# A two-phase attention and feed-forward kernel: one weight reload issued later and from another queue, denser weight conversion between the phases, and another order of the last products

## The chip, the cores and the metric

The kernel runs on one core of one Trainium2 chip. The metric is the device time of one execution, in microseconds (us), as a median of several runs. The core has a matrix engine (PE, with its weight loads shown apart as PEld), VectorE (DVE), ScalarE (ACT), GpSimd (POOL) and SyncE (SP, which here only issues DMA transfers). Each engine works through its own instructions in their order and waits for the others by semaphores.

## The reference

Sliding-window attention with a few sink columns, then a feed-forward layer over all 3072 tokens:

```python
scores = scale * np.matmul(q, k.transpose(0, 1, 3, 2))      # 4 x 8 heads, 768 x 768, head size 64
scores = np.where(is_sink | in_window, scores, -1e9)
a = softmax(scores)
x = np.matmul(a, v)            # -> 3072 tokens x 512
h = x @ w_in                   # 512 -> 2048
r = np.maximum(h, 0.0)
g = s * (r * r) + b
out = g @ w_out                # 2048 -> 512
```

The weights arrive as 8-byte floats, which the kernel turns into float32 itself, and every float32 number is split into a high and a low part for the matrix engine.

## The kernel before

**Two phases.** In the first, the tokens go through in 8 chunks of 384: attention and the first layer together. For each chunk, 16 column blocks of `h` (f = 0 to 15) are made from 12 matmuls each (L692), ACT takes each block through Relu into a tile `g` (L698), and each pair of blocks is stored to DRAM (L700, from SP). `g` has three buffers, so the ACT instruction of a pair waits until the store of the pair three before it has landed. In the second phase the 3072 tokens go through in 6 blocks (`blk`) of 512, and each block in 8 steps (`q`), together 48 units `n`. A unit loads a pair of `h` blocks back (`load`, L778, from SP), squares and combines it on ACT and DVE into the operands `gA` and `gH` (`prep`, L780 to L799), and PE multiplies them with seven combinations of the second layer's weights into seven accumulators `Q[j]` (`products`, L817): 42 matmuls, in the order j = 0, 1, 5, 6, 4, 2, 3. j = 0, 1 and 3 take `gA`, the other four `gH`. `prep(n+1)` is written ahead of `products(n)`.

**The weights of the second layer.** Step q needs a tile `v{q}` of converted weights. Six of the eight pairs are converted early, among the attention chunks. Three of them stay in SBUF; the other three (q = 3, 4, 5) are stored to DRAM (`spilled`) and fetched back when the attention's buffers are free: `reload(q)`, L763, 1792 KB each, called here reload 3, 4 and 5. The last two raw weight words (q = 6 and 7, 1024 KB each, called raw 6 and raw 7) are loaded (L709, SP) at that moment into the tiles that reloads 4 and 5 will later fill, and converted while PE works on the last chunk's `h`. The conversion of one (`w2_steps`) is two ACT instructions on the raw words (L235, L236), three DVE instructions (L237, L239, L241), DVE differences (L718) and casts on ACT (L721, L734). It is written in four pieces, one behind each `h` block from the third on (`late_w2`, in the loop over the last chunk), and reload 4 or 5 stands behind each conversion.

**What sets the order.** A scheduler sets the order of instructions on each engine from the order in which they are written and from its own estimates, so pieces that are written later may still stand between others. SP's transfers start in SP's order.

**The end.** In the last step of a block, `drain` adds the accumulators up: `u1` is a copy of `Q[0]` (ACT, L834), `o1`'s left half is `Q[1] + u1`, `u1 += Q[5]`, `u3 = Q[6] + u1`, `u1 += Q[4]`, `o2`'s right half is `Q[4] + u3`, `o1`'s right half is `Q[2] + u1` (DVE, all by the helper at L830), and `o2`'s left half is `u3 - Q[3]`, in the last block in two parts with a bank each (L822). In the last block each part is sent off by `put` (L862, SP) as soon as it is written.

Of the kernel before, what the change touches and what calls it, by code (L numbers as in the profile page):

```python
# [8 lines left out]
F32 = mybir.dt.float32  # L9
F32R = mybir.dt.float32r  # L10
I32 = mybir.dt.int32
U32 = mybir.dt.uint32
U8 = mybir.dt.uint8
AF = mybir.ActivationFunctionType
ALU = mybir.AluOpType
AX = mybir.AxisListType

P = 128
B, H, S, D = 4, 8, 768, 64
# [15 lines left out]
EARLY, SPILL = 3, 3  # L35
HD = DM // 2
NP = NF // 2
TB = 4 * P
NT = B * S // TB
# [6 lines left out]
def tile_kernel(ctx, tc, qT, kT, k0, v, vsk, n_sink, window, w1, w2, s, b, out):  # L46
    nc = tc.nc
# [6 lines left out]
    def ps(name):  # L54
        return pools[0].tile([P, 512], F32, tag="a", name=name)
# [3 lines left out]
    kept = kept_cm.__enter__()  # L59
# [54 lines left out]
    rel, rel1, low, upp, kix, snk, tmp, tm2 = (sc0[:, j, :] for j in range(8))  # L114
# [97 lines left out]
    weight, raws, last = {}, {}, {}  # L212
# [12 lines left out]
    def scratch(name, dt=F32):  # L225
        return kept.tile([P, 2, DM], dt, tag="cs", name=name, bufs=2)

    def float_steps(raw, scratch, pin=lambda x: x, up=2.0 ** -111):


        lo, hi = raw[..., 0], raw[..., 1]
        t = []
        sc, ve = nc.scalar, nc.vector
        return [
            lambda: pin(sc.activation(lo, lo.bitcast(U32), AF.Copy, scale=2.0 ** -29)),  # L235
            lambda: pin(sc.mul(hi.bitcast(F32), hi.bitcast(F32), up)),  # L236
            lambda: pin(ve.tensor_scalar(out=t.append(scratch()) or t[0], in0=hi, scalar1=3, scalar2=None,  # L237
                                         op0=ALU.logical_shift_left)),
            lambda: pin(ve.scalar_tensor_tensor(out=t[0], in0=hi, scalar=-0x80000000, in1=t[0],  # L239
                                                op0=ALU.bitwise_and, op1=ALU.bitwise_or)),  # L240
            lambda: pin(ve.tensor_tensor(out=hi, in0=t[0], in1=lo, op=ALU.add))]  # L241
# [463 lines left out]
    spilled = {q: dram.tile([P, 7, 2, HD], F32R, tag=f"wd{q}", name=f"wd{q}") for q in range(EARLY, EARLY + SPILL)}  # L705
# [31 lines left out]
    def halves_of(t):  # L737
        return t[:, :3], t[:, 3:]
# [15 lines left out]
    def second_layer(p2):  # L754


        def late_v(q, shape=(P, 7, 2, HD), dt=F32R):
            return p2.tile(list(shape), dt, tag=f"v{q}", name=f"v{q}")

        def reload(q):  # L760
            t = late_v(q)
            wc[q] = halves_of(t)
            nc.gpsimd.dma_start(t, spilled[q])  # L763

        for q in range(2):
            load_w2(NP - 2 + q, late_v(EARLY + 1 + q, [P, 2, 2 * DM], I32))
        reload(EARLY)
        wc[NP - 2] = halves_of(late_v(NP - 2))
        wc[NP - 1] = (p2.tile([P, 3, 2, HD], F32R, tag="vb", name="vb"), kept_w(0, "vt", [P, 4, 2, HD], F32R))

# [30 lines left out]
        Q = {}  # L801

        def products(n):
            blk, q = units[n]
            left = ready.pop(n)
            right = [wc[q][0][:, j] for j in range(3)] + [wc[q][1][:, j] for j in range(4)]
            last, end = q == NP - 1, blk == NT - 1
            for j in (0, 1, 5, 6, 4, 2, 3):
                if q == 0:
                    Q[j] = ps("Q").rearrange("p (r f) -> p r f", r=2)  # L810
                    if end and j == 3:
                        Q[3, 1] = ps("Q").rearrange("p (r f) -> p r f", r=2)
                for rb in range(2):
                    parted = end and j == 3
                    bank = Q[3, 1] if parted and rb else Q[j]
                    for i, (gi, wi) in enumerate(((0, 0), (0, 1), (1, 0))):
                        nc.tensor.matmul(bank[:, rb], left[j][:, gi, rb * P:(rb + 1) * P], right[j][:, wi],  # L817
                                         start=(q == 0 and (rb == 0 or parted) and i == 0),
                                         stop=(last and (rb == 1 or parted) and i == 2))
                    if last and parted:  # L820
                        o = D["o"][1]
                        nc.vector.tensor_tensor(out=o[:, rb, :HD], in0=D["u3"][:, rb], in1=bank[:, rb], op=ALU.subtract)  # L822
                        put(blk, 1, o, slice(rb, rb + 1), slice(0, HD))
                if last and not parted:
                    drain(blk, j)

        D = {}

        def drain(blk, j):
            add = lambda o, x, y, op=ALU.add: nc.vector.tensor_tensor(out=o, in0=x, in1=y, op=op)  # L830
            u = lambda name: kept.tile([P, 2, HD], F32, tag="x0", name=name, bufs=2)
            if j == 0:
                D["u1"] = u("u1")
                nc.scalar.copy(D["u1"], Q[0])  # L834
                D["o"] = [kept.tile([P, 2, DM], F32, tag="x1", name="ot", bufs=2) for _ in range(2)]
            o1, o2 = D["o"]
            end = blk == NT - 1
            lo, hi, both = slice(0, HD), slice(HD, DM), slice(0, 2)
            if j == 1:
                add(o1[:, :, lo], Q[1], D["u1"])  # L840
                if end:
                    put(blk, 0, o1, both, lo)
            if j == 5:
                add(D["u1"], Q[5], D["u1"])
            if j == 6:
                D["u3"] = u("u3")
                add(D["u3"], Q[6], D["u1"])
            if j == 4:
                add(D["u1"], Q[4], D["u1"])
                add(o2[:, :, hi], Q[4], D["u3"])  # L850
                if end:
                    put(blk, 1, o2, both, hi)
            if j == 2:
                add(o1[:, :, hi], Q[2], D["u1"])
                put(blk, 0, o1, both, hi if end else slice(0, DM))
            if j == 3:
                nc.vector.tensor_tensor(out=o2[:, :, lo], in0=D["u3"], in1=Q[3], op=ALU.subtract)
                put(blk, 1, o2, both, slice(0, DM))

        def put(blk, half, o, rb, cols):  # L860
            rows = out[blk * TB + half * HT:blk * TB + (half + 1) * HT, cols].rearrange("(r p) e -> p r e", p=P)
            nc.sync.dma_start(rows[:, rb], o[:, rb, cols])  # L862
# [193 lines left out]
    todo = [(max(t * t1 - LEAD, 0.3), f) for t, f in enumerate(plain)] + [(t2 - 2, constants3), (t2, scalars)]  # L1056
# [17 lines left out]
    reload, load, prep, products, n_units = second_layer(p2)  # L1074
    late = {}

    def late_w2(q, a, z):
        if a == 0:
            late[q] = w2_steps(q)
        for f in late[q][a:z]:  # L1080
            f()

    todo = []
    for j in range(2):
# [2 lines left out]
    for m in range(n, len(steps)):  # L1087
        steps[m]()
        if m % PIECES < PIECES - 1:
            continue  # L1090
        m = m // PIECES - n_last
        if m == NF // 2:
            go = out_of_range()
        if m >= 2 and todo:
            todo.pop(0)()
        if m >= NF - 3:
            load(m - (NF - 3))
    prep(0)
# [57 lines left out]
```

## Time and profile before

| what | us |
|---|---|
| median of 3 runs | 726.9 (726.4 to 727.88) |
| the profiled execution | 726.22 |
| its span, first to last instruction | 724.5 |
| PE busy | 696.1 (96%) |
| PE weight loads busy | 659.1 (91%) |
| DVE busy | 575.6 (79%) |
| ACT busy | 531.7 (73%) |
| POOL busy | 130.5 (18%) |

The profiled execution is 1.7 us longer than its span and 0.7 us under the median of the runs. PE is busy nine tenths of nearly every slice of the span; the shares of the others say little about a single stage. The change touches two stages: the turn from phase 1 to phase 2, about 436 to 487 us from the span's start, and the last 12 us. For these the views to read are who waited for whom on PE, the chain of work that ended last, the instructions in order of time, and the transfers with their time to landing.

### The profile page before, as it was taken

How to read it: one execution, taken by the hardware profiler on the slowest of the kernel's cores; microseconds unless marked ns; L12 is line 12 of the kernel's file. 1: busy time of each engine (PE TensorE's matmuls, PEld its weight loads, DVE VectorE, ACT ScalarE, POOL GpSimd, SP SyncE). 2: the span in 40 equal slices, each digit the busy share in tenths (PEclk: the TensorE clock that was granted, in tenths of full speed). 3: DMA queues.
4: the chain of work that ended last, by engine and by line, in shares of the span. 5: the costliest groups of instructions: out<-in, count | busy, mean ns of one | idle time of the engine just before them, and what ended most of it. 6: DMA issues, size and time to landing. Idle time of an engine off the chain costs nothing.

```text
span 724.5 us, 14198 instructions
## 1 busy us (share of the span) xinstructions
PE 696.1 (96%) x4858; PEld 659.1 (91%) x4858; DVE 575.6 (79%) x1458; ACT 531.7 (73%) x1229; POOL 130.5 (18%) x295
## 2 busy tenths in 40 slices
PE   9889999999999999999999999999999999999995
PEld 5667789999999998898899999999999999999995
DVE  7798976977887887877977862858888888888883
ACT  5898788789789789888888853846566665756561
POOL 4000122424424424424324310000000000000000
PEclk9999999999999999999999999999999999999998
DMA  8942254366456456453454318863534444443521
GB/s 206 410 148 84 67 180 149 107 209 219 133 178 222 141 169 244 126 175 112 136 185 131 108 67 327 267 221 117 154 109 124 138 118 146 117 146 117 151 84 62
DMA packets 61185, 114.13 MB, mean 158 GB/s; under 512 B 8368, under 2 KB 37168, under 8 KB 58288
## 3 DMA queue, kind: packets, MB, share of 16 engines
q1 hardware_dynamic: 59584, 107.43, 46.1%
q0 software_dynamic: 432, 5.51, 2.2%
q8 instruction: 40, 0.66, 0.4%
q14 instruction: 41, 0.34, 0.1%
q10 hardware_dynamic: 1088, 0.20, 0.1%
HBM read 76.16 MB, written 36.96 MB: 156 GB/s over the span
## 4 chain that ended last, share of the span: by engine, by line
PE 40%; DVE 14%; ACT 7%; DMA 7%; issue 4%; POOL 0%; ACTq 0%; DVEq 0%; POOLq 0%; SPq 0%
PE Q L817 21%; PE h L692 14%; DMA gs<-gs 5%; PE o L405 2%; DVE gA L796 2%; DVE sm L344 1%; DMA kraw<-in_kT 1%; ACT sm L350 1%; DVE hl L369 1%; ACT gs L785 1%; DVE gH L798 1%; DVE kl L321 1%; DVE u L830 1%; DVE qs L320 1%; ACT g L698 1%
## 5 line engine op out<-in xcount | busy, mean ns | idle before, releaser
L692 PE MATMUL h<-x,w 128*128 128x384 f32 x1536 | 306.4, 343 | 4.4 <-DVE negm L344 2.9
L692 PEld LDWEIGHTS h<-x,w 128*128 128x128 f32 x1536 | 261.9, 188 | 11.6 <-DVE negm L344 4.6
L817 PE MATMUL Q<-v,gH 128*128 128x256 f32 x1008 | 128.5, 283 | 0.3 <-DVE ot L830 0.2
L817 PEld LDWEIGHTS Q<-v,gH 128*128 128x128 f32 x1008 | 124.2, 192 | 0.7 <-issue 0.6
L785 ACT ACTIVATE gs<-gs,sbu 128x1024 f32<-128x1024 f32 x48 | 55.3, 1151 | 70.1 <-DMA gs<-gs 63.2
L817 PE MATMUL Q<-v,gA 128*128 128x256 f32 x756 | 99.0, 283 | 1.1 <-DVE gA L796 1.1
L350 ACT ACTIVATE sm<-sm,negm 128x264 f32<-128x264 f32 (+1 forms) x144 | 72.8, 506 | 32.3 <-DVE negm L344 28.8
L817 PEld LDWEIGHTS Q<-v,gA 128*128 128x128 f32 x756 | 94.4, 192 | 1.4 <-DVE gA L796 1.3
L698 ACT ACTIVATE g<-h 128x384 f32<-128x384 f32 x128 | 62.2, 490 | 18.6 <-PE h L692 13.3
L352 POOL COPY psk<-sm 128x24 f32<-128x24 f32 x144 | 37.0, 259 | 177.8 <-ACT sm L350 176.0
L369 DVE TENSOR_TENSOR hl<-tp,hl 128x256 fp32r<-128x256 f32 (+1 forms) x144 | 57.9, 403 | 9.7 <-ACT hl L368 8.7
L344 DVE CUSTOM_DVE_ANT_0 sm<-sc,msk 128x264 f32<-128x264 f32 (+1 forms) x144 | 59.0, 410 | 3.7 <-PE sc L340 1.2
L798 DVE TENSOR_TENSOR gH<-gs,gH 128x1024 fp32r<-128x1024 f32 x48 | 58.4, 1217 | 2.8 <-ACT gH L797 2.8
L795 ACT ACTIVATE gA<-gs,sbu 128x512 fp32r<-128x512 f32 x96 | 53.7, 607 | 8.3 <-PE Q L817 8.3
L405 PE MATMUL o<-hl,vv 128*128 128x128 f32 (+2 forms) x352 | 56.5, 278 | 3.4 <-DVE hl L369 1.7
L797 ACT CAST gH<-gs 128x1024 fp32r<-128x1024 f32 x48 | 50.0, 1041 | 12.1 <-DVE gs L790 7.0
L796 DVE SCALAR_TENSOR_TENSOR gA<-gs,sbu,gA 128x512 fp32r<-128x512 f32 x96 | 54.8, 611 | 0.0
L414 DVE TENSOR_TENSOR xm<-o,y 64x384 f32<-64x384 f32 x48 | 26.6, 555 | 34.3 <-ACT y L413 31.0
L787 DVE SCALAR_TENSOR_TENSOR gs<-gs,sbu 128x256 f32<-128x256 f32 x48 | 23.1, 482 | 37.9 <-ACT gs L785 37.7
L368 ACT CAST hl<-tp 128x256 fp32r<-128x256 f32 (+1 forms) x144 | 50.7, 353 | 1.7 <-PE tp L364 1.0
L405 PEld LDWEIGHTS o<-hl,vv 128*128 128x128 f32 (+1 forms) x352 | 40.3, 164 | 6.1 <-DVE hl L369 2.7
L339 PE MATMUL sc<-kh,qs 128*128 128x264 f32 (+1 forms) x144 | 40.2, 279 | 0.8 <-ACT g L698 0.6
(180 smaller groups left out, 1154.5 us busy)
## 6 DMA issues: line engine op xcount, KB each, us to landing
gs<-g SPq DMA_DIRECT2D x64, 384.0 KB, 3.1
gs<-gs SPq DMA_DIRECT2D x48, 512.0 KB, 4.2
kraw<-in_kT SPq DMA_DIRECT2D x32, 264.0 KB, 2.8
wraw<-in_w SPq DMA_DIRECT2D x8, 1024.0 KB, 11.4
vraw<-in_w SPq DMA_DIRECT2D x6, 1024.0 KB, 5.4
wd<-v SPq DMA_DIRECT2D x3, 1792.0 KB, 6.4
v<-wd POOLq DMA_DIRECT2D x3, 1792.0 KB, 9.5
out<-ot SPq DMA_DIRECT2D x10, 512.0 KB, 3.2
```

The source lines that it names most:

```text
L344: nc.vector.tensor_tensor_reduce(out=sm[:, :n], in0=sc[:, :n], in1=m, scale=-0.125, scalar=BIG, op0=ALU.add, op1=ALU.min, accum_out=negm[: ...
L350: nc.scalar.activation(sm[:, :n], sm[:, :n], AF.Exp, bias=negm[:, uu], scale=-1.0, accum_out=pp.zz[:, i, hh:hh + 1])
L368: nc.scalar.copy(hi, tp[:, a:z])
L369: nc.vector.tensor_tensor(out=lo, in0=tp[:, a:z], in1=hi.bitcast(F32), op=ALU.subtract)
L405: nc.tensor.matmul(hd.o[:m, q0:q0 + n * P], hd.vv[:, kb, :m], hd.hl[:, t, c0 * P:(c0 + n) * P], start=(hd.n == 0), stop=(end and t == 0))
L692: nc.tensor.matmul(h[:, :CH], w_in(f, wi)[:, cc * P:(cc + 1) * P], k.x[xi][:, cc, :], start=(i == 0), stop=(i == len(order) - 1))
L698: nc.scalar.activation(g["r"][:, f % 2], h[:, :CH], AF.Relu, scale=1.0 / WUP)
L785: nc.scalar.activation(g[:, 0], g[:, 0], AF.Square, scale=root_ap)
L795: nc.scalar.activation(o[:, :, 0], x, AF.Identity, bias=b1_ap, scale=1.0)
L796: stt(out=o[:, :, 1], in0=x, scalar=b1_ap, in1=o[:, :, 0].bitcast(F32), op0=ALU.add, op1=ALU.subtract)
L798: nc.vector.tensor_tensor(out=H[:, :, 1], in0=S, in1=H[:, :, 0].bitcast(F32), op=ALU.subtract)
L817: nc.tensor.matmul(bank[:, rb], left[j][:, gi, rb * P:(rb + 1) * P], right[j][:, wi], start=(q == 0 and (rb == 0 or parted) and i == 0), s ...
```

## The change

Four things. The reload of q = 3 is no longer issued by POOL before the last chunk; it is issued from ACT's queue, behind the first ACT instruction on raw 7 (and as plain float32, on both sides). The pieces of the last two conversions are called denser: one behind the third `h` block, then two behind each of the next three. In the last block the products go in the order j = 0, 5, 6, 4, 1, 2, 3. And there `Q[1]` is copied by ACT and added by POOL, from a tile with three parts, instead of by DVE.

```diff
-            lambda: pin(sc.activation(lo, lo.bitcast(U32), AF.Copy, scale=2.0 ** -29)),
+            lambda: last.update(low=pin(sc.activation(lo, lo.bitcast(U32), AF.Copy, scale=2.0 ** -29))),
...
-        def reload(q):
+        def reload(q, queue=nc.gpsimd):
             t = late_v(q)
             wc[q] = halves_of(t)
-            nc.gpsimd.dma_start(t, spilled[q])
+            queue.dma_start(t.bitcast(F32), spilled[q].bitcast(F32))
...
-        reload(EARLY)
...
-            for j in (0, 1, 5, 6, 4, 2, 3):
+            for j in (0, 5, 6, 4, 1, 2, 3) if end else (0, 1, 5, 6, 4, 2, 3):
...
             if j == 0:
-                D["u1"] = u("u1")
+                if blk == NT - 1:
+                    us = kept.tile([P, 3, 2, HD], F32, tag="x0", name="us", bufs=2)
+                    D["u1"], D["sum"], D["q1"] = (us[:, i] for i in range(3))
+                else:
+                    D["u1"] = D["sum"] = u("u1")
...
             if j == 1:
-                add(o1[:, :, lo], Q[1], D["u1"])
                 if end:
+                    nc.scalar.copy(D["q1"], Q[1])
+                    nc.gpsimd.tensor_tensor(out=o1[:, :, lo], in0=D["q1"], in1=D["u0"], op=ALU.add)
                     put(blk, 0, o1, both, lo)
+                else:
+                    add(o1[:, :, lo], Q[1], D["u1"])
             if j == 5:
-                add(D["u1"], Q[5], D["u1"])
+                D["u0"], D["u1"] = D["u1"], D["sum"]
+                add(D["u1"], Q[5], D["u0"])
...
             f()
+        if q == NP - 1 and a == 0:
+            with tc.issue_after(last["low"].ins):
+                reload(EARLY, nc.scalar)
...
-        if m >= 2 and todo:
-            todo.pop(0)()
+        for _ in range(2 if 3 <= m < 6 else int(m >= 2)):
+            if todo:
+                todo.pop(0)()
```

How it moves instructions. **ACT, from the end of raw 6's conversion** (`v_6284` and `v_6286` are raw 6 and raw 7, `vb` and `vt` the converted tiles of q = 7, L785 the square of a loaded unit). Before:

```order
L734 CAST v_6290<-vT 128x4x256
L698 ACTIVATE g<-h 128x384
L785 ACTIVATE gs<-gs,sbu 128x1024
L698 ACTIVATE g<-h 128x384
L235 ACTIVATE v_6286<-v_6286 128x1024
L236 ACTIVATE v_6286<-v_6286,sbu 128x1024
L698 ACTIVATE g<-h 128x384
L785 ACTIVATE gs<-gs,sbu 128x1024
L698 ACTIVATE g<-h 128x384
L795 ACTIVATE gA<-gs,sbu 128x2x256
L795 ACTIVATE gA<-gs,sbu 128x256
L721 CAST vb<-v_6286 128x2x256
```

The changed kernel, from the same cast:

```order
L734 CAST v_6288<-vT 128x4x256
L235 ACTIVATE v_6286<-v_6286 128x1024
L236 ACTIVATE v_6286<-v_6286,sbu 128x1024
L763 DMA v_6440<-wd_117 128x3584
L698 ACTIVATE g<-h 128x384
L721 CAST vb<-v_6286 128x2x256
L721 CAST vb<-v_6286 128x256
L698 ACTIVATE g<-h 128x384
L734 CAST vt<-vT 128x4x256
```

Raw 7's conversion stands directly behind raw 6's, reload 3 in the middle of it, and the squares of units 1 and 2 and unit 0's `gA` have moved behind it all.

**ACT, the last `h` blocks and the first units.** From the cast of `vt`, the last of the conversion. Before:

```order
L734 CAST vt<-vT 128x4x256
L795 ACTIVATE gA<-gs,sbu 128x2x256
L795 ACTIVATE gA<-gs,sbu 128x256
L698 ACTIVATE g<-h 128x384 x2
L797 CAST gH<-gs 128x4x256
L698 ACTIVATE g<-h 128x384 x2
L797 CAST gH<-gs 128x4x256
L785 ACTIVATE gs<-gs,sbu 128x1024
```

The changed kernel, from the row behind that cast:

```order
L698 ACTIVATE g<-h 128x384 x4
L794 ACTIVATE gA<-gs,sbu 128x2x256
L698 ACTIVATE g<-h 128x384
L794 ACTIVATE gA<-gs,sbu 128x256
L784 ACTIVATE gs<-gs,sbu 128x1024 x2
L698 ACTIVATE g<-h 128x384
L796 CAST gH<-gs 128x4x256
L698 ACTIVATE g<-h 128x384
```

The four L698 are blocks 8 to 11, the single ones 12, 13 and 14: unit 0's second `gA`, the squares of units 1 and 2 and unit 0's `gH` now stand behind the L698 of block 12, which waits for the store of blocks 6 and 7 to land; the last L785 of before (unit 3) follows later.

**DVE and SP at the end** (`u` and `us` are the sums, `ot` the parts of the output, Q the accumulators). DVE before:

```order
L830 TENSOR_TENSOR ot<-Q,u_9446 128x2x256
L830 TENSOR_TENSOR u_9446<-Q,u_9446 128x512
L830 TENSOR_TENSOR u_9471<-Q,u_9446 128x512
L830 TENSOR_TENSOR u_9446<-Q,u_9446 128x512
L830 TENSOR_TENSOR ot<-Q,u_9471 128x2x256
L830 TENSOR_TENSOR ot<-Q,u_9446 128x2x256
L822 TENSOR_TENSOR ot<-u_9471,Q 128x256 x2
```

DVE in the changed kernel:

```order
L829 TENSOR_TENSOR us<-Q,us 128x512
L829 TENSOR_TENSOR u_9463<-Q,us 128x512
L829 TENSOR_TENSOR us<-Q,us 128x512
L829 TENSOR_TENSOR ot<-Q,u_9463 128x2x256
L829 TENSOR_TENSOR ot<-Q,us 128x2x256
L821 TENSOR_TENSOR ot<-u_9463,Q 128x256 x2
```

SP's five stores of the last block in the changed kernel, with what each waits for:

```order
L869 DMA out<-ot 128x2x256 [waits DVE_49]
L869 DMA out<-ot 128x2x256 [waits Pool_49]
L869 DMA out<-ot 128x2x256 [waits DMAHW6_49,DVE_49]
L869 DMA out<-ot 128x256 [waits DMAHW7_49,DVE_49]
L869 DMA out<-ot 128x256 [waits DVE_49]
```

DVE's first sum is gone from the head of the row; the store that waits for POOL's sum is SP's second, where before it was the first and waited for DVE, and three stores stand behind it.

## Rows read from the trace of the kernel before

**Rows 1.** The page's head line: span and instructions.
```profile
span 724.5 us, 14198 instructions
```
**Rows 2.** Who PE waited for, 430 to 726 us: total us, times, longest.
```profile
PE Q L817 <- DVE gA L796: 1.1, 1, 1.1
```
**Rows 3.** The chain that ended last, 465 to 486 us: start us, us, what.
```profile
471.52 1.15 DVE gH L798
472.68 6.63 DMA gs<-gs
...
483.37 0.76 DVE gA L796
```
**Rows 4.** Instructions in order of time, 456 to 469 us, POOL and SP: start us, us.
```profile
456.91 0.54 POOL L763 DMA_DIRECT2D v<-wd  x1 [19.50 <-DVE v L718]
...
458.83 0.51 SPq L700 DMA_DIRECT2D gs<-g  x1
...
468.71 0.53 POOL L763 DMA_DIRECT2D v<-wd  x1 [11.26 <-DVE vb L718]
```
**Rows 5.** Transfers issued at 447.45, 456.91, 458.83, 466.70, 468.71, 484.53: last number us to landing.
```profile
gs<-gs SPq DMA_DIRECT2D x1, 512.0 KB, 6.2
...
v<-wd POOLq DMA_DIRECT2D x1, 1792.0 KB, 9.5
...
gs<-g SPq DMA_DIRECT2D x1, 384.0 KB, 8.4
...
gs<-g SPq DMA_DIRECT2D x1, 384.0 KB, 2.7
...
v<-wd POOLq DMA_DIRECT2D x1, 1792.0 KB, 8.5
...
gs<-gs SPq DMA_DIRECT2D x1, 512.0 KB, 4.2
```
**Rows 6.** Transfers by queue, 441 to 448 us: packets, MB, share of 16 engines.
```profile
q0 software_dynamic: 128, 1.84, 69.9%
q1 hardware_dynamic: 131, 0.95, 37.6%
```
**Rows 7.** ACT's instructions in order of time, 445 to 473 us.
```profile
453.65 1.15 ACT L785 ACTIVATE gs<-gs,sbu 128x1024 f32<-128x1024 f32 x1 [2.65 <-DMA gs<-gs]
...
458.70 1.14 ACT L235 ACTIVATE v<-v 128x1024 int32<-128x1024 uint32 x1
...
472.76 0.49 ACT L698 ACTIVATE g<-h 128x384 f32<-128x384 f32 x1 [1.10 <-PE h L692]
```
**Rows 8.** PE's instructions in order of time, at the turn and at the end.
```profile
457.87 14.85 PE L692 MATMUL h<-x,w 128*128 128x384 f32 x84
472.57 1.59 PE L817 MATMUL Q<-v,gA 128*128 128x256 f32 x12
...
716.26 0.88 PE L817 MATMUL Q<-vt,gA 128*128 128x256 f32 x6
```
**Rows 9.** ACT and DVE in order of time, 712 to 719 us.
```profile
712.86 0.59 ACT L834 COPY u<-Q 128x512 f32<-128x512 f32 x1 [4.36 <-PE Q L817]
...
713.64 0.69 DVE L830 TENSOR_TENSOR ot<-Q,u 128x512 f32<-128x512 f32 x1 [3.85 <-ACT u L834]
...
714.43 2.28 DVE L830 TENSOR_TENSOR u<-Q,u 128x512 f32<-128x512 f32 x3
...
...
717.83 0.74 DVE L822 TENSOR_TENSOR ot<-u,Q 128x256 f32<-128x256 f32 x2
```
**Rows 10.** SP's issues of the last three stores, in order of time.
```profile
717.94 0.59 SPq L862 DMA_DIRECT2D out<-ot  x1
...
719.12 0.45 SPq L862 DMA_DIRECT2D out<-ot  x1
```
**Rows 11.** The last store, issued at 719.12: KB, us to landing.
```profile
out<-ot SPq DMA_DIRECT2D x1, 128.0 KB, 3.4
```
**Rows 12.** POOL's additions of two inputs by line and shape: busy us, mean ns.
```profile
L438 POOL TENSOR_TENSOR x<-xm,x 128x384 fp32r<-128x384 f32 x24 | 28.8, 1198 | 32.8 <-ACT x L437 32.8
```

## The prediction

> **What bounds the kernel now.** The head of the page gives the span, 724.5 us [rows 1]. I read next who PE waited for from the last chunk to the end: one wait counts, 1.1 us for DVE's `gA` [rows 2]; from 457.87 on PE runs without a gap through the last `h` blocks into the second phase at 472.57 [rows 8]. So PE is the bound, and all that the turn between the phases can give back is that 1.1 us. The chain of waits says whose it is [rows 3]: DVE ends `gH` of unit 0 at 472.66, which frees the buffer for unit 3; the load of unit 3 goes out at 472.68 and takes 6.63 us; ACT's square of unit 3 stands ahead of unit 2's `gH` and `gA` in ACT's order, so it holds them until the landing at 479.31; unit 2's `gA` is ready at 484.13, 4.8 us after it. The same kind of load takes 4.2 us when no reload is under way [rows 5]. Reload 5 left at 468.71 [rows 4] and needed 8.5 us [rows 5], so it lay across that load. PE wanted the low half of `gA` 1.1 us before 484.1, at about 483.0.
>
> At the other end PE stops at 717.14 [rows 8]; what follows is DVE's sums, from 713.64 to 718.57 [rows 9], SP's last issue at 719.12 [rows 10] and its landing 3.4 us later [rows 11], at 722.5; 2.0 us of closing work remain.
>
> **Reload 3 leaves 436.7, and raw 6 and 7 come in alone.** That frees the stores and unit 0's load behind them in SP's queue. ACT waited 2.65 us for that load [rows 7], which took 6.2 us [rows 5]; at 4.2 for a free one it lands 2 us sooner. PE waits for nothing there, so by itself this is worth 0; it moves ACT's work. The DMA that is now ACT's costs ACT an issue of about half a microsecond (SP's took 0.45 to 0.59 [rows 4, 10]). Behind it ACT soon waits for DVE's three steps on raw 7 (L237, L239, L241), which hide it; without that cover reload 5 and the stores behind would go later by as much.
>
> **The denser conversion.** Raw 7's first ACT step stands directly behind raw 6's last cast: 2 us from the earlier load, and about 1.7 us for two L698 and a square that stood between (0.49 and 1.15 [rows 7], overlapping by a tenth or more). So it starts near 455.0, not 458.70 [rows 7]. From there to reload 5 took 10.0 us (468.71 - 458.70) [rows 4, 7]; I estimate 2 us of it for the square and the `gA` that were mixed in, so reload 5 goes out near 463, 5.7 us sooner. Reload 4 goes 2 us sooner than 456.91, near 454.9, and reload 3 near 457.2, behind two ACT steps. All three now lie in the 18 us before the turn; each alone takes 8.5 to 9.5 us to land [rows 5].
>
> **The load of unit 3.** Its buffer is freed by unit 0's `gH`, and that work has moved behind the conversion and behind the L698 of blocks 8 to 13. PE makes a block in 14.85 / 7 = 2.12 us [rows 8], and block 15's L698 ran at 472.76 [rows 7], so block 12 is ready at 466.4. Behind it ACT has a half `gA` (0.6, half a square), two squares (1.15 each), block 13, and the cast of `gH`, as wide as a square: 0.5 + 0.6 + 2.3 + 0.5 + 1.15 = 5.05 [rows 7], done at 471.5; DVE's 1.15 for `gH` [rows 3] ends at 472.65, the same as now. If reload 5 has landed by then (463 + 8.5 = 471.5), unit 3's load takes 4.2 us, lands at 476.9, and unit 2's `gA` is ready 4.8 us later, at 481.7, ahead of 483.0. PE's 1.1 us goes. The price of a delay: PE takes 0.121 us a matmul (2016 of them from 472.57 to 717.14 [rows 8]), so it wants unit 0's low `gH` 14 matmuls in, at 474.25. ACT may be 1.6 us late; beyond that every microsecond is one on PE.
>
> **What can be late there.** Block 12's L698 waits for the store of blocks 6 and 7, which now leaves behind block 7's L698, and that stands behind raw 7's casts: near 462, not 458.83 [rows 4]. Such a store lands in 2.7 us when alone, but took 8.4 under reload 4, 0.8 us behind it (467.2 against 466.4) [rows 4, 5]. Alone it lands at 464.7; behind all three reloads at 463 + 8.5 + 0.8 = 472.3. I take 468.3: reloads 3 and 4 and unit 2's load, 4.2 MB, at the 2.79 MB in 7 us of [rows 6] are 10.5 us, from 457 to 467.5, and 0.8; reload 5 needs time to begin, and the store is queued first. Block 12 is then 1.9 us late, 0.3 over the slack. **The turn: -1.1 + 0.3 = -0.8 us**, with bounds -1.1 (store by 468.0) and +3.2 (472.3: 5.9 - 1.6 = 4.3, less 1.1).
>
> From 441 to 448 the reload on POOL's queue and the transfers on SP's, nearly all raw words, moved 128 and 131 packets, one for one [rows 6]. The Trainium skill ("DMA: Bandwidth & Descriptors", Queues, rings and completion order) says that each DMA engine takes turns between its queues packet by packet; the row agrees. By that rule a third queue (ACT's) leaves SP's small packets a third of the turns while reloads 3 and 4 overlap, which speaks against this change, and the store would land behind the last reload: the +3.2 end, a rival below.
>
> **The end.** The new order takes DVE's first sum out of the row, so that it begins with `Q[5]`. `Q[0]`'s copy ends at 713.45, as now; six matmuls take 0.72 us, so `Q[5]` is ready at 712.86 + 0.72 = 713.58, and DVE starts at 713.64 the sum that it started at 714.43. It stays 0.79 us ahead [rows 9]: its last sum ends at 717.8, still after PE's last product. But SP's second store now waits for POOL. `Q[1]` is the fifth, ready at 712.86 + 4 x 0.72 = 715.74; ACT's copy takes 0.59 [rows 9], to 716.33. An addition of 512 columns on POOL isn't in the trace; 384 took 1.2 us [rows 12], so it is between 1.2 and, by width, 1.6; I take 1.45, nearer to the width, since it works column by column. POOL ends at 717.8. SP then issues four stores 0.59 apart (717.94 to 719.12 for three [rows 10]) or a little less: the last near 717.85 + 3 x 0.55 = 719.5, where it went at 719.12, +0.4. Against it, the last store took 3.4 us [rows 11], and one three times its size 2.7 [rows 5]; up to 0.7 may come back, and I take 0.2. **The end: +0.2 us**, bounds -0.6 (POOL at 1.2, landing at 2.7) and +1.0 (POOL held to 2 us beside DVE, landing as now). The copy and the sum that the change adds cost nothing else: ACT and POOL have no work left there.
>
> **Sum.** 724.5 - 0.8 + 0.2 = 723.9, -0.6 us: 725.6 for the profiled execution (726.2), and 726.9 - 0.6 = 726.3 on the median. The profiled execution is 0.7 us under the median, so the difference is what carries over.
>
> **The rivals.** *Both gains in full:* the store of blocks 6 and 7 lands by 468.0, PE's 1.1 us goes entirely, and the end gives 0.5: -1.6, 725.3. For it: the store may be through before reload 5 begins to move. Against: PE can give no more than 1.1, and POOL must be quick. *The reloads crowd the turn, and it gets slower:* three reloads within 8 us keep SP's queue back, the store of blocks 6 and 7 lands only behind reload 5, at 472.3, ACT stands at block 12, and unit 0's `gH` comes 4.3 us late: -1.1 + 4.3 + 0.2 = +3.4, 730.3. It decides from a landing at 469.1 on, where the gain is eaten up, and reaches 1.45 us slower at 470.4. For it: the store under reload 4 landed behind it, and one-for-one packets; against: reload 5 starts 6 us after the others and may find the store ahead of it. *The change doesn't do what it says:* reload 5 is still under way at 472.7, the wait near 484 stays, and only the end counts: +0.2, 727.1.
>
> **How the numbers follow.** Forecast (turn -1.1 to +0.2, end -0.3 to +0.7; 725.5 to 727.6): 0.45. Both in full: 0.20. Crowded: 0.25, from 727.6 to 731. Nothing at the turn: 0.10. A measurement can tell about 0.2%, 1.45 us: faster is under 725.45, slower over 728.35. Faster: most of the 0.20 and the forecast's edge: 0.20. Slower: the crowded case beyond 470.4, 0.20, and 0.02 for an end that goes badly: 0.22. Same: 0.58. The range reaches down to the full gain, 725.0, and up to a crowded store near 471, 729.2.
>
> **What would show it.** Right: no wait of PE for `gA` near 484; unit 3's load lands in under 5 us; reload 5 issued near 463; DVE's last sum ends near 717.8 and SP's second store goes right behind POOL's addition, near 717.9. Wrong: a wait of ACT's L698 for a store between 466 and 472 and of PE for `gH` between 472 and 478 (crowded); a load of unit 3 of over 6 us (the wait stays); an addition of over 2 us on POOL, or a last store that goes out before 719.1, makes the end another than I summed.

## The result, and the profile after

| | before | after |
|---|---|---|
| median | 726.9 us (726.4 to 729.31, 5 runs) | 734.84 us (732.58 to 738.15, 5 runs) |
| ratio | 1 | 1.0093, 95% interval 1.0064 to 1.0121 |
| profiled execution: time, span | 726.2, 724.5 us | 738.15, 736.4 us |

The kernel is 0.9% slower by the ratio, 7.9 us on the medians (the ratio and its interval are estimated from all the runs; the medians alone would give 1.0109). The forecast was 726.3, with a range up to 729.2: wrong in sign and outside the range. What came is the rival in which the reloads crowd the turn, at more than twice its price of 3.4 us.

Who PE waited for from 425 us to the end, after (total us, times, longest); [rows 2] had one line, 1.1 for `gA`:

```profile
PE Q L816 <- ACT gH L796: 5.0, 1, 5.0
PE Q L816 <- DVE gH L797: 1.3, 2, 0.8
PE Q L816 <- DVE gA L795: 0.3, 1, 0.3
```

The old wait for unit 2's `gA` is gone, as the sum had it. In its place stands unit 0's `gH`, five times as long. PE in order of time there (start us, us), which answers to the second row of [rows 8]:

```profile
476.08 1.45 PE L816 MATMUL Q<-v,gA 128*128 128x256 f32 x10 [0.29 <-DVE gA L795]
482.50 0.79 PE L816 MATMUL Q<-v,gH 128*128 128x256 f32 x2 [4.96 <-ACT gH L796]
484.06 4.28 PE L816 MATMUL Q<-v,gH 128*128 128x256 f32 x22 [0.77 <-DVE gH L797]
```

Before, the same 24 products with `gH` ran without a gap:

```profile
473.99 3.04 PE L817 MATMUL Q<-v,gH 128*128 128x256 f32 x24
```

The 22 matmuls of the last row of after take 4.28 us; at the 0.121 of [rows 8] they would take 2.7. The stretches say why (us, busy time of PE, PEld, DVE, ACT and POOL, then the granted clock, DMA share, GB/s):

```profile
476.00:480.00 4.00, 1.45 (x10) 1.25 (x10) 0.51 (x2) 1.83 (x4) 0.00 (x0) 1.00 0.48 177
480.00:484.00 4.00, 0.79 (x2) 0.50 (x2) 3.87 (x9) 4.00 (x8) 0.00 (x0) 0.55 0.27 99
484.00:488.00 4.00, 3.94 (x21) 3.94 (x22) 2.60 (x5) 1.16 (x2) 0.00 (x0) 0.60 0.58 143
488.00:492.00 4.00, 4.00 (x35) 4.00 (x35) 1.24 (x4) 2.46 (x3) 0.00 (x0) 1.00 0.62 219
```

PE stood for most of 477.5 to 484, and the granted clock fell to its lower level, half, until about 487. In the kernel before it is 1.00 throughout this stretch. So PE's standstill seems to be paid twice: as a wait, and in slow matmuls behind it. An experiment below tests the second.

Why `gH` is late is in ACT's order of time:

```profile
473.76 0.88 ACT L698 ACTIVATE g<-h 128x384 f32<-128x384 f32 x2 [6.99 <-DMA gs<-g]
...
478.17 0.49 ACT L698 ACTIVATE g<-h 128x384 f32<-128x384 f32 x1 [2.94 <-DMA gs<-g]
...
478.96 2.17 ACT L784 ACTIVATE gs<-gs,sbu 128x1024 f32<-128x1024 f32 x2
...
481.41 1.04 ACT L796 CAST gH<-gs 128x1024 fp32r<-128x1024 f32 x1
```

ACT stands 6.99 us at blocks 10 and 11 for the store of blocks 4 and 5, then 2.94 us at block 12 for the store of blocks 6 and 7, and unit 0's `gH` is in line behind. Those two stores, unit 2's load between them, and reload 5 (last number us from issue to landing):

```profile
gs<-g SPq DMA_DIRECT2D x1, 384.0 KB, 16.7
...
gs<-gs SPq DMA_DIRECT2D x1, 512.0 KB, 18.7
...
gs<-g SPq DMA_DIRECT2D x1, 384.0 KB, 13.3
...
v<-wd POOLq DMA_DIRECT2D x1, 1792.0 KB, 10.0
```

A store that took 2.7 us alone and 8.4 under one reload [rows 5] takes 13 to 17 here.

PE's stretch gives one measure of the turn that does not depend on when an execution reaches it: the time from unit 0's first product to unit 7's first. Seven units of 42 products at 0.12 us are 35.28 us without any wait. Before it was 509.22 - 472.57 = 36.65, after 44.08. The turn costs 7.4 us more. Of the rest of the profiled difference (11.9), 2.7 us is the start: PE began the second phase at 475.29 against 472.57. The kernel below with the change at the turn alone began at 472.39, so this is not the turn's change; the kernels below began anywhere from 472.4 to 474.8. Another 0.7 lies at the end, and 1.1 between unit 7 and the last products, most of it in two short stands of PE near 649 and 693 us.

### The profile page after: what moved, and what is told of

It is laid out like the page before. It is cut to its first block, busy times and chain, and to the rows that moved or that the text cites. A ratio compares the mean times of both kernels' runs of the same rounds, so it can differ in the third digit from the quotient of the medians.

```text
span 736.4 us, 14199 instructions
## 1 busy us (share of the span) xinstructions
PE 700.9 (95%) x4858; PEld 662.3 (90%) x4858; DVE 575.6 (78%) x1457; ACT 532.9 (72%) x1230; POOL 131.4 (18%) x295
## 4 chain that ended last, share of the span: by engine, by line
## 5 line engine op out<-in xcount | busy, mean ns | idle before, releaser
L816 PE MATMUL Q<-v,gH 128*128 128x256 f32 x1008 | 131.9, 286 | 6.5 <-ACT gH L796 5.0
L816 PEld LDWEIGHTS Q<-v,gH 128*128 128x128 f32 x1008 | 126.3, 194 | 7.8 <-ACT gH L796 5.2
L816 PE MATMUL Q<-v,gA 128*128 128x256 f32 x756 | 100.6, 284 | 0.3 <-DVE gA L795 0.3
L698 ACT ACTIVATE g<-h 128x384 f32<-128x384 f32 x128 | 61.9, 486 | 26.5 <-PE h L692 12.2
L795 DVE SCALAR_TENSOR_TENSOR gA<-gs,sbu,gA 128x512 fp32r<-128x512 f32 x96 | 54.9, 612 | 11.1 <-ACT gA L794 11.1
```

The lines of the kernel that those rows point to most:

```text
L698: nc.scalar.activation(g["r"][:, f % 2], h[:, :CH], AF.Relu, scale=1.0 / WUP)
L795: stt(out=o[:, :, 1], in0=x, scalar=b1_ap, in1=o[:, :, 0].bitcast(F32), op0=ALU.add, op1=ALU.subtract)
```

## The experiments

Each kernel's measure of the turn beside its time:

| kernel | turn, us | median, us | ratio to before (95%) |
|---|---|---|---|
| before, beside each of the others | 36.65 | 726.7 to 727.5 | 1 |
| after | 44.08 | 734.84 | 1.0093 (1.0064 to 1.0121) |
| the turn's change alone | 43.54 | 733.31 | 1.0091 (1.0066 to 1.0117) |
| reload 3 moved, alone | 36.94 | 727.03 | 0.9995 (0.9982 to 1.0007) |
| denser conversion, alone | 36.64 | 725.62 | 0.9981 (0.9955 to 1.0006) |
| the end's change alone | 38.93 | 728.49 | 1.0013 (0.9989 to 1.0036) |
| turn, rows of 2 KB | 40.04 | 730.93 | 1.0047 (1.0028 to 1.0065) |
| turn, four block buffers | 36.51 | 728.5 | 1.0021 (1.0001 to 1.0040) |
| turn, reload 3 made to wait | 44.19 | 734.56 | 1.0089 (1.0063 to 1.0114) |
| turn, PE kept at work | 47.70 | 737.38 | 1.0136 (1.0106 to 1.0166) |
| turn, one reload held | 36.54 | 730.14 | 1.0029 (1.0010 to 1.0048) |
| turn, two reloads held | 41.89 | 732.35 | 1.0068 (1.0054 to 1.0081) |
| before, reload 5 held | 36.22 | 725.67 | 0.9992 (0.9968 to 1.0017) |
| denser conversion, reload 5 held | 35.26 | 724.38 | 0.9967 (0.9946 to 0.9988) |

A turn is read from one execution and a median from at least four, so they needn't agree. How far a single turn can be off, the kernel with the end's change alone shows: its code at the turn is that of before, and yet its turn is 2.3 us longer. Its load of unit 3 took 7.1 us (6.6 before), PE stood 0.15 and 1.5 us for unit 2's `gA`, and the granted clock fell behind that:

```profile
484.88 2.45 PE L817 MATMUL Q<-v,gA 128*128 128x256 f32 x10 [1.50 <-DVE gA L796]
484.00:488.00 4.00, 3.12 (x15) 3.12 (x16) 3.96 (x9) 2.22 (x4) 0.00 (x0) 0.62 0.32 84
```

Beside the experiments the runs of the kernel before itself lay between 725.4 and 733.5 us. So the times decide, and a turn that is 2 us longer in one trace doesn't by itself show a loss.

The theory after the result: three reloads in ten microseconds keep SP's queue back, ACT stands at a block's L698 for a store, and unit 0's `gH` waits behind it in ACT's order. Rivals: the denser steps hold ACT up by themselves; reload 3's move alone does it; it lies at the end or in the start.

**The parts.** The first kernel has the change at the turn and the end as before. The second keeps of it only reload 3's move, by the first edit here; the third only the denser steps, by the second edit, with reload 3 behind raw 6 and 7 on POOL's queue as before; the fourth has both edits and the new end.

```diff
-        for _ in range(2 if 3 <= m < 6 else int(m >= 2)):
-            if todo:
-                todo.pop(0)()
+        if m >= 2 and todo:
+            todo.pop(0)()
```

```diff
+        reload(EARLY)
...
-        if q == NP - 1 and a == 0:
-            with tc.issue_after(last["low"].ins):
-                reload(EARLY, nc.scalar)
```

> The change at the turn alone, with the end as before. Theory (the reloads crowd the turn): reloads 3, 4 and 5 leave POOL's and ACT's queues within 10 us, SP's stores of h blocks land 12 to 17 us after their issue instead of 3 to 8, ACT stands at an L698 for them, unit 0's gA and gH come late, PE waits some 5 us for gH and goes on at half clock for some 7 us. So this kernel loses nearly all that the changed kernel lost: 732.5 to 735, store of blocks 6 and 7 landing after 475. Rival (the loss lies at the end, or at the start as a shift of the whole program): 727 to 729, with PE's wait at the turn under 2 us.

> Reload 3 on ACT's queue behind raw 7's first step, conversion steps as sparse as before, end as before. Theory (crowding): reloads 3 and 4 overlap from about 457, reload 5 follows near 468, so the queue of SP is held back until about 478; the store of blocks 6 and 7 (issued near 459) lands after 469, ACT stands at L698, PE waits 1 to 5 us: 728.5 to 733. Rival (the denser steps put the loss there: ACT's work for unit 0 moved behind the conversion): nothing but the reload has moved, so 726 to 728, with no wait of PE for gH.

> The denser conversion alone: reload 3 stays on POOL's queue at its early place, end as before. Theory (crowding): only reloads 4 and 5 lie in the 18 us before the turn, both on POOL's queue, and the store of blocks 6 and 7 lands 8 to 10 us after an issue near 462, at 470 to 472: 726 to 729.5, with a wait of PE for gH under 2 us. Rival (denser steps themselves): ACT's half gA, squares and blocks stand behind the casts whatever the reloads do, so most of the loss is here: 731 to 735.

> The change at the end alone, the turn as before. Theory: what the changed kernel's trace shows (PE's end to the end of the span 8.06 us, against 7.36) is the end's share: +0.7, so 727.2 to 728.0. Rival (the end as it was forecast): +0.2, 726.7 to 727.3. Rival (the end is where the time went): 731 or more.

Measured: the turn alone carries the whole loss (1.0091 against 1.0093). The end alone is 1.0013 (0.9989 to 1.0036), 728.49 us median, a little over what was expected. But neither part of the turn costs anything that can be told by itself, which the theory had not expected of reload 3's move (728.5 to 733, measured 727.03); the denser steps alone came out at 725.62, under the expected 726. Both traces, ACT in order of time, first with reload 3 moved alone:

```profile
471.10 0.49 ACT L698 ACTIVATE g<-h 128x384 f32<-128x384 f32 x1 [4.54 <-DMA gs<-g]
471.49 1.11 ACT L794 ACTIVATE gA<-gs,sbu 128x512 fp32r<-128x512 f32 x2
472.50 0.48 ACT L698 ACTIVATE g<-h 128x384 f32<-128x384 f32 x1
472.87 1.04 ACT L796 CAST gH<-gs 128x1024 fp32r<-128x1024 f32 x1
```

and with the whole change at the turn:

```profile
473.86 0.49 ACT L698 ACTIVATE g<-h 128x384 f32<-128x384 f32 x1 [5.24 <-DMA gs<-g]
474.25 0.50 ACT L794 ACTIVATE gA<-gs,sbu 128x256 fp32r<-128x256 f32 x1
474.65 2.17 ACT L784 ACTIVATE gs<-gs,sbu 128x1024 f32<-128x1024 f32 x2
476.72 0.47 ACT L698 ACTIVATE g<-h 128x384 f32<-128x384 f32 x1
477.09 1.04 ACT L796 CAST gH<-gs 128x1024 fp32r<-128x1024 f32 x1
```

ACT stands at block 12 in both, 4.5 and 5.2 us, so the crowding is in both. In the first, the sparse steps let block 7 pass earlier: the store of blocks 6 and 7 leaves at 457.75 and lands at 471.0, and `gH`'s cast, nearly next behind block 12, ends at 473.9, before PE wants it at 474.5. In the second the store leaves at 462.4, the cast ends 4.2 us later, and PE waits 4.21 us. Of these 4.2, 2.8 are the later block 12 and 1.5 what the scheduler now puts between (half a `gA` and the squares of units 1 and 2 in the place of one `gA`). So the loss is an interaction: crowding makes the store late, the denser steps send the store off later, and with both in the code the scheduler puts more work behind it. With the denser steps alone it does not: there the store leaves at 460.61 and lands in 7.2 us, the squares of units 1 and 2 stand ahead of block 9, and `gH`'s cast ends at 470.3.

**Is it the stand at block 12?** Four buffers for the pairs of blocks, with reloads and order unchanged (for six, with which ACT would wait for none of these stores, SBUF is too small: 3.3 KB a partition would be left where another pool of tiles needs 5.6, so that kernel has no result):

```diff
-                g["r"] = kept.tile([P, 2, CH], F32, tag="g", name="g", bufs=3)
+                g["r"] = kept.tile([P, 2, CH], F32, tag="g", name="g", bufs=4)
```

> The turn's change alone, with four buffers for the pairs of h blocks in place of three, so that block 12 waits for the store of blocks 4 and 5 and not for that of blocks 6 and 7; reloads and instruction order stay. Theory (ACT's stand at block 12 for the store of blocks 6 and 7, with unit 0's gH behind it, is what PE waits for): stores and loads land as late as with the turn's change alone (11 to 14 us), but ACT passes block 12 near 467.5, unit 0's gH comes near 473 to 474 behind unit 2's load (469.96) and its square, PE's wait for gH falls from 4.2 to under 1 us, the clock stays: 726 to 728.5. Rival (the loads of units 1 and 2 and the denser steps hold gH back by themselves): 731 to 735.

The store of blocks 6 and 7 takes 11.1 us as before, and ACT passes block 12 all the same:

```profile
467.87 0.49 ACT L698 ACTIVATE g<-h 128x384 f32<-128x384 f32 x1 [1.11 <-DMA gs<-g]
...
471.58 1.04 ACT L796 CAST gH<-gs 128x1024 fp32r<-128x1024 f32 x1
```

PE's waits for `gH` are gone; its one wait is 0.98 us for `gA`, and the turn takes 36.51 us. This shows the link from the store over ACT to PE. The time is 728.5 in the median, at the upper edge of what was expected: the loss falls from 0.9% to 0.2%. The ten runs spread from 725.92 to 731.28; the profile is of one at 726.76, and what the longer ones have is not shown.

**Which store?** Reload 3 left at 454.14, ahead of ACT's two steps on raw 7, and 0.4 us ahead of the store of blocks 4 and 5. Here ACT first writes two elements of its target from the second step's result:

```diff
+            if behind is not None:
+                nc.scalar.copy(t[:1, 0, 0, :2], behind)
             queue.dma_start(t.bitcast(F32), spilled[q].bitcast(F32))
...
-                reload(EARLY, nc.scalar)
+                reload(EARLY, nc.scalar, raw2[q][:1, 0, :2, 1].bitcast(F32))
```

> The turn's change alone, with reload 3 made to wait for raw 7's second step: ACT first writes two elements of its target from that step's result. In the kernel without this the reload left 2.2 us ahead of that step and 0.4 us ahead of the store of blocks 4 and 5, which it held for 12.5 us. Theory (the store of blocks 6 and 7 sets the end, with ACT's order behind it): the store of blocks 4 and 5 lands in 3 to 5 us and ACT's first stand is gone, but blocks 6 and 7 still land after 471 and PE still waits 3 us or more: 730.5 to 733. Rival (the first store that is caught decides): the time falls to 726.5 to 728.5.

The store of blocks 4 and 5 now lands in 2.7 us and ACT's first stand is gone. That of blocks 6 and 7 takes 16.3 us, and PE waits 4.9: the turn is 44.19 (time 734.56, a little over what was expected). So of the two stores it is the later one that counts.

**Rows or bytes?** The same turn with the late weights' copies laid out so that a reload's rows are 2 KB:

```diff
-    spilled = {q: dram.tile([P, 7, 2, HD], F32R, tag=f"wd{q}", name=f"wd{q}") for q in range(EARLY, EARLY + SPILL)}
+    spilled = {q: dram.tile([7, P, 2, HD], F32R, tag=f"wd{q}", name=f"wd{q}").rearrange("j p t f -> p j t f") for q in range(EARLY, EARLY + SPILL)}
```

> The turn's change alone, with the copies of the late weights laid out in DRAM so that a reload's rows are 2 KB and not 14336 bytes (as many bytes, same places, same order on every engine). Theory (SP's small packets get one turn for each large packet of a reload, so a tenth of the bytes): with rows of 2 KB SP's queue gets a third to a half, the store of blocks 4 and 5 lands 4 to 8 us after its issue (12.5 in the kernel with the turn's change alone), that of blocks 6 and 7 before 470, PE's wait for gH falls under 2 us: 726 to 729. Rival (the chip's transfers are full, so bytes count and not rows): the stores land as late as before, 732 to 735.

Transfers by queue from 459 to 465 us (packets, MB, share of 16 engines): q0 is POOL's queue, q10 ACT's, q1 SP's. First the turn's change alone, then with rows of 2 KB:

```profile
q0 software_dynamic: 122, 1.75, 72.1%
q10 hardware_dynamic: 52, 0.52, 20.2%
q1 hardware_dynamic: 131, 0.20, 8.9%
```

```profile
q10 hardware_dynamic: 510, 1.03, 47.8%
q0 software_dynamic: 202, 0.83, 33.5%
q1 hardware_dynamic: 319, 0.49, 21.7%
```

With large rows SP's queue gets 131 of 305 packets but 0.20 of 2.47 MB, 8%. The Trainium skill ("DMA: Bandwidth & Descriptors", Queues, rings and completion order) has each DMA engine take turns between its queues packet by packet, and the rows agree: POOL's and SP's queues had nearly as many turns (122 and 131; ACT's transfer ends within the stretch), and bytes go by the size of what a turn moves. With reload 3 moved alone, where two reloads and SP's queue were all under way from 462 to 464 us, the three queues had 29, 28 and 29 packets. With small rows SP gets 21% of the bytes, PE's waits for `gH` fall from 5.3 to 2.3 us, and about half of the turn's loss comes back (40.04). The store of blocks 6 and 7 still takes 8.7 us, and 730.93 misses the 726 to 729 expected. So the step from rows of 14 KB to 2 KB gives back half, and not all of that need be the rows' doing: reload 5 also left 7 us later there, at 470.98, when the store of blocks 6 and 7 was nearly in. That two reloads have two turns to SP's one may account for the rest, but was not tried by itself.

**The clock.** 40 more products on PE where it waits, into a bank of their own:

```diff
+                if n == 0 and j == 5:
+                    W = ps("W")
+                    for _ in range(40):
+                        tc.keep_in_program_order(nc.tensor.matmul(W[:, :HD], left[0][:, 0, :P], right[0][:, 0], start=True, stop=True))
```

> The turn's change alone, with 40 more products of 256 columns on PE ahead of unit 0's first gH product, into a bank of their own; they are 4.8 us of work in the place of PE's 4.2 us wait and add nothing to the result. Theory (PE's standstill brings the granted clock to half for some 7 us behind it, which costs about 2.6 us on top of the wait): the clock stays at full speed, 22 gH matmuls take 2.9 us and not 5.06, and the kernel gets faster by 2 to 3 us although PE has more to do: 730 to 731.5. Rival (the lower clock has another cause, or costs nothing): 733 to 734.

PE in order of time, the turn alone and then with the extra products:

```profile
478.19 0.50 PE L816 MATMUL Q<-v,gH 128*128 128x256 f32 x2 [4.21 <-ACT gH L796]
479.74 5.06 PE L816 MATMUL Q<-v,gH 128*128 128x256 f32 x22 [1.06 <-DVE gH L797]
```

```profile
474.97 4.96 PE L811 MATMUL W<-v,gA 128*128 128x256 f32 x40
480.83 0.50 PE L820 MATMUL Q<-v,gH 128*128 128x256 f32 x2 [0.90 <-ACT gH L796]
482.39 2.89 PE L820 MATMUL Q<-v,gH 128*128 128x256 f32 x22 [1.06 <-DVE gH L797]
```

The stretch from 480 to 484 us in the first and in the second:

```profile
480.00:484.00 4.00, 4.00 (x20) 4.00 (x21) 2.28 (x4) 0.84 (x1) 0.00 (x0) 0.50 0.72 180
```

```profile
480.00:484.00 4.00, 2.12 (x15) 1.91 (x16) 4.00 (x9) 3.49 (x6) 0.00 (x0) 1.00 0.36 108
```

The granted clock is 0.50 and 1.00, and 22 matmuls take 5.06 and 2.89 us: the standstill brings the clock down. That it would be a gain is not shown. The kernel is 4 us slower, not 2 to 3 faster: in its profile the store of blocks 4 and 5 lands 4 us later than in the other, `gH` comes 2.6 later, and PE then waits 3.1 us for unit 2's `gA`. The changed kernel had its stores as late (16.7 and 13.3 us, here 16.1 and 13.4) with the same code at the turn as the turn's change alone (12.5 and 11.4), so this may be the execution and not the edit; why is open.

**Reloads out of the way.** A reload is held by two elements that POOL writes into its target from unit 3's square. PE wants reload 4 near 493 and reload 5 near 498 us.

```diff
-        todo.append(lambda j=j: reload(EARLY + 1 + j))
...
+            g3 = raw[3][:1, 0, 0, :2] if n == 2 else None
             prep(n + 1)
+            if n == 2:
+                reload(EARLY + 1, behind=g3)
+                reload(EARLY + 2)
```

> The turn's change alone, with reloads 4 and 5 held behind unit 3's square (POOL writes two elements from its result into reload 4's target), so that only reload 3 lies ahead of the turn. Theory (it is the number of reloads that lie together, not the move of reload 3 or the denser steps): the stores of blocks 4 to 7 land within 9 us, ACT stands under 2 us, PE has no wait for gH; reloads 4 and 5 land near 488 and 497, where PE wants them near 493 and 498: 724 to 726. Rival (the denser steps hold unit 0 up by themselves): 729 or more; and if reload 5 lands behind 498, up to 2 us more.

The edit did less than that text says: nothing held reload 5, and the scheduler sent it off at 464.0, so only reload 4 was held. It also did more: in this kernel and the next the scheduler puts unit 1's square ahead of block 12 and unit 2's behind unit 0's `gH`, so the order on ACT is not that of the turn's change alone. In the profiled execution the store of blocks 6 and 7 lands in 3.4 us and the turn is 36.54, near before. But the runs spread from 725.84 to 731.51 with a median of 730.14, and the profile is of the shortest; so this kernel does not decide. With `behind=g3` on the last line too, both are held:

> As the kernel with reloads 4 and 5 held, but with both of them really held: POOL writes two elements from unit 3's square into each one's target. (In that kernel only reload 4 was; the scheduler sent reload 5 off at 464.0.) So reload 3 alone lies ahead of the turn. Theory (reloads side by side keep SP's stores back): every store of blocks 4 to 11 lands within 5 us of its issue once reload 3 is through near 463, ACT's stands at L698 stay under 1.5 us, unit 3's load lands in under 5 us, PE waits for nothing at the turn; reload 4 leaves near 479 and lands near 487, reload 5 lands near 495, PE wants them near 493 and 498: 724 to 726, with a smaller spread than the 725.8 to 731.5 of the kernel with one held. Rival (the moved reload 3 or the denser steps cost by themselves): 727 or more; and if reload 5 lands behind 498, up to 2 us more.

The first 20 us are as the theory has them: PE waits for nothing from 474 to 493, the stores of blocks 6 to 11 land in 2.75 to 3.35 us, unit 3's load in 4.2. And yet it is 732.35. The same thing now happens 20 us later. The two reloads leave together, at 479.25 and 479.94, and unit 5's load follows at 482.38 (transfer, then packets by queue from 482 to 488 us, then who PE waited for):

```profile
gs<-gs SPq DMA_DIRECT2D x1, 512.0 KB, 11.6
```

```profile
q0 software_dynamic: 179, 2.35, 95.0%
q1 hardware_dynamic: 45, 0.09, 3.9%
```

```profile
PE Q L818 <- issue: 2.4, 1, 2.4
PE Q L818 <- DVE gA L797: 1.5, 1, 1.5
```

ACT there:

```profile
494.06 1.15 ACT L786 ACTIVATE gs<-gs,sbu 128x1024 f32<-128x1024 f32 x1 [8.25 <-DMA gs<-gs]
...
496.05 1.12 ACT L796 ACTIVATE gA<-gs,sbu 128x512 fp32r<-128x512 f32 x2
```

The load takes 11.6 us instead of 4.2, unit 4's `gA` (496.05) stands behind unit 5's square (494.06) in ACT's order, and PE stands 4 us and goes on at half clock. Two reloads on one queue do much of what three on two did (a turn of 41.89 against 43.54).

**One reload at a time, away from the loads.** Reload 5 alone held, by the same lines without the one for `EARLY + 1`, in the kernel before and with the denser conversion:

> The kernel before, with reload 5 alone held behind unit 3's square, conversion as sparse as before. Theory (PE's 1.1 us at unit 2's gA is the load of unit 3 under reload 5, and nothing else): the load lands in 4.2 to 5 us, the wait goes, and the time is that of the denser conversion with the same hold, 1 to 1.5 us under before: 725 to 726.3. Rival (the denser conversion brings a gain of its own): the same as before, 726.3 to 727.5.

> The denser conversion alone, with reload 5 held until unit 3's square (POOL writes two elements of its target from the square's result), which is a try at a better kernel. Theory (reload 5 slows unit 3's load from 4.2 to 6.6 us, and that is PE's last wait of 1.1 us): unit 3's load lands in under 5 us, reload 5 leaves near 478 and lands near 488, 11 us before PE wants it, PE waits for nothing at the turn: 1 us less than the denser conversion alone, 724 to 725.5. Rival (something else is late next, a load of units 4 or 5 under the moved reload): no gain, 725 to 727.

With the denser conversion unit 3's load lands in 4.5 us, PE waits for nothing at the turn, and the turn is 35.26: no wait left. At 724.38 (0.9967, 0.9946 to 0.9988) this is faster than both kernels, by a third of a percent against before and clear of its interval. The turn accounts for 1.4 of the 2.3 us between the medians; the rest is not traced, and the profile is of one of the longer runs (726.71, second phase from 474.76). With the sparse steps half a microsecond of wait stays and the gain (0.9992) is inside its interval.

**The end.** DVE, POOL and SP at the end, after:

```profile
727.61 1.28 POOL L845 TENSOR_TENSOR ot<-us 128x512 f32<-128x512 f32 x1 [260.91 <-ACT us L844]
...
727.75 3.28 SPq L869 DMA_DIRECT2D out<-ot  x5
728.26 0.74 DVE L821 TENSOR_TENSOR ot<-u,Q 128x256 f32<-128x256 f32 x2
```

From the start of PE's last six products to the end of the span it is 8.94 us after and 8.95 with the end's change alone, against 8.24 before [rows 1, 8]. That looks like +0.7. But the experiments that have the old end show 8.07 to 9.2, so one execution can't tell; the timed comparison is +0.1% with an interval on both sides of nothing.

## Why the prediction was wrong

**Right.** PE's wait for unit 2's `gA` went, with unit 3's load in 4.8 us and no reload across it, as the sum had it; but the load left at 479.72 and not 472.68, and PE was as late. The new places were found well: in the kernel with the turn's change alone, whose second phase begins at 472.39 as before, reload 4 left at 455.70 (454.9 forecast), reload 5 at 463.76 (463), the store of blocks 6 and 7 at 462.37 (462); reloads 3 and 4 were both in by 466.71 (467.5). The last is partly luck: the sum counted from 457 and reload 3 left at 454.14. From block 12 to the end of `gH`'s cast ACT took 4.3 us (5.05). The order of what follows on ACT and the price, each microsecond beyond the slack one on PE, held too.

**The step that failed** is the landing of the store of blocks 6 and 7: "I take 468.3 ... reload 5 needs time to begin, and the store is queued first." It landed at 473.76, 0.2 behind reload 5. The sum gave SP's queue its bytes in turn with the reloads, as if all 4.2 MB went at one common rate. But SP moved 8% of the bytes while reloads ran, so the store of blocks 4 and 5 landed at 467.06 and unit 2's load only at 469.96, both ahead of this store in the same queue (0.9 MB in all), and by then reload 5 was moving. So the store was not next in line when reloads 3 and 4 ended. Reload 5 did need time to begin, but from 468 to 473 SP's queue again got only 0.31 MB beside its 1.73. The sum also took the store of blocks 4 and 5 as gone by then; it left 0.4 us behind reload 3.

**The rule that was set aside.** The prediction cited the turns packet by packet and took from them the +3.2 end. [rows 6] agreed with it, 128 packets against 131, but they were of 14336 and mostly 8192 bytes there (1.84 and 0.95 MB), so they hid how little small rows get. With the rival at one in four, the trace's best evidence was underweighted.

**The rival's price was short too.** It had the landing at 472.3 and +3.2 at the turn. With the turn's change alone the turn cost 6.9: PE's waits of 4.21 and 1.06, less the 1.4 that before lost here, are 3.9; the other 3.0 lie behind the waits, 2.5 of them in 40 matmuls at the lower clock (5.06 and 2.69 us where they take 2.89 and 2.32 at the full one), which no term of any case held. Block 12's delay by the measured landing (473.76 - 466.4 = 7.4, less 1.6) would have given 5.8 of wait: the chain behind the landing was sized within 0.6.

**"Reload 3 near 457.2, behind two ACT steps"** was wrong as well: it left 454.14, ahead of both. It waited for nothing they produce. By the experiment that made it wait, this changed nothing that the times can tell (1.0089 against 1.0091).

**The end** (+0.2 forecast): POOL's addition took 1.28 us (1.45), DVE's last sum ended 0.77 us sooner against PE's end (0.79), SP's second store went out at POOL's end as the text said. What the whole gives is within -0.1 and +0.4% of nothing and can't be told closer.

**What stays open:** how much of the 4.2 us the order on ACT would cost by itself (read from two traces, not tried); why the kernels with four buffers and with one reload held, and before itself, have runs of 725 to 726 and of 731; why the stores are later in some executions, as where PE is kept at work. PE's wait at unit 2 with the clock behind it, long in the trace of the end's change and short in that of before, may be one reason for the spread, but no two traces of one kernel show it.

## What to carry over

A transfer with large rows, on POOL's queue or ACT's, left a queue of small rows 4 to 15% of the bytes here, in stretches of 5 or 6 us; before moving one, list what is queued behind it in every queue, who waits for those, and whether two of them now overlap. When a wait's price is worked out, add what the clock costs behind the standstill, here 2.5 us on 5. A reload that is wanted late may be sent off late, but one at a time: a crowd of two, moved 20 us on, cost three quarters as much (1.0068 against 1.0091).

## What the runs showed of the hardware

- A DMA issued by ACT was not held by ACT's earlier work, on which it doesn't depend: it left at 454.14, 1.2 us before the first and 2.2 us before the second of raw 7's steps, which stood ahead of it in program order; with two elements written into its target it left at 458.70, behind both. So the order of an engine's program held here for its work and not for the DMA that it issues.
- With rows of 2 KB, reload 5 left POOL's queue only at 470.98, right behind reload 4's landing (470.67); with rows of 14336 bytes it left at 463.76, 3 us ahead of that landing (466.71).
- After PE stood 4 to 6 us, in one piece or two, the granted clock was at half for about 7 us, in four kernels and at two places. One standstill of 1.0 to 1.1 us (before, denser conversion, four buffers) left it at full; two of 1.3 and 1.1 us within three (rows of 2 KB) brought it down too, 0.79 and 0.78 in the two stretches of 4 us from 476, and so did 0.15 and 1.5 us (the end's change alone), 0.62 from 484 to 488.
